# Letting GpSimd take q×E, k/E, the carried state's masked copy and the squares, under a newly drawn order of steps

## The chip, the cores and the metric

The kernel runs on one core of a Trainium2 chip. The metric is the time of one execution on the device in microseconds, as a median of runs. A core has five engines that run side by side, each in its own order: TensorE (PE in the profile), VectorE (DVE), ScalarE (ACT), GpSimd (POOL) and SyncE (SP), which here only issues transfers.

## The reference

Two layers, one after the other. The first is a recurrence over 768 places in 4 batches and 8 heads of width 48, with a complex decay for each place and channel:

```python
mag = np.sqrt(a_re * a_re + a_im * a_im)
scale = np.minimum(mag, 0.999) / (mag + 1e-06)
a_re_n, a_im_n = (a_re * scale, a_im * scale)
for t in range(S):                                  # S = 768
    new_re = ar * S_re - ai * S_im
    new_im = ar * S_im + ai * S_re
    kv = np.einsum('bhd,bhe->bhde', k[:, :, t], v[:, :, t])
    S_re, S_im = (new_re + kv, new_im)
    y[:, :, t] = np.einsum('bhd,bhde->bhe', q[:, :, t], S_re)
```

The second takes y as x, 3072 rows of 384 channels, through a gated feed-forward layer with a gated residual:

```python
g = x @ w_gate                                      # 384 to 1536
gelu = 0.5 * g * (1.0 + erf(g * inv_sqrt2))
ffn_out = gelu * (x @ w_val) @ w_out                # 1536 to 384
res_gate = 1.0 / (1.0 + np.exp(-(x @ w_res)))
return x + res_gate * ffn_out
```

## The kernel before

The sequence is cut into 6 chunks of 128 places, which lie on the 128 partitions. A unit is one chunk of one or two batches; there are 14 units (0 to 13), of one chunk each for units 0, 1, 12 and 13 and of two for the others. For each unit three functions record steps.

`prepare` loads a_re, a_im, q, k and v by SyncE's queue (`load`, L374). From a_re and a_im it makes the logarithm of the decay and its angle: `ln`, `exp`, `tai` (t times a_im, L398), `sq` (the square, L400 or L402), `lnb`, `la`, `lh`, `ll`, and `atan`. The running sums over the 128 places are products on TensorE with a triangle of ones (`cumL`, `cumT`, L360). To keep float32 accuracy each summand is split into a half-precision part and a rest: `lh` and `ll`, `th` and `tl` (L444). ScalarE turns the sums into E (`pexpE`) and its inverse Ei (`pexpI`), and with `round`, `fr`, `abs` and `sin` into cosine and sine, CS. Then `qe` makes q×E and k×Ei (k over E), in bfloat16 (L470), and `feat` multiplies both with CS to the features of width 96 (L475). These are transposed, on TensorE with a copy out of PSUM (`peT`, L492, and `cpT`, L334 or L335) in units 0 to 7, by SyncE's queue (`dT`, L484) later. The angle's last row goes from chunk to chunk by a transfer on GpSimd's queue (`carry`, L432 and L438).

`attend` makes the query-key products (`qk`, L522), masks them (`am`, L525), multiplies with v and adds the carried state (`av`, L534 and L536), and copies the result to x. The carried state is updated: `kv` on TensorE, `U` (L552) adds the old state, and two masked copies are made, Gb in bfloat16 (L554) for the next product and Gf in float32 (L559) for the next update.

`forward` is the second layer: x transposed, `gv` (L592), `gelu` (L597) on ScalarE, `h` (L598) on VectorE, `res` (L607), `tanh` (L609), `out` (L618), `ot` (L622), and `otx` (L625), the sum with x, before the store (L627).

The steps are not issued as they are recorded. All 1450 have a number; ORDER lists them in the order of issue, over all units and engines, and PLACE gives the engine of those steps that may run on more than one (`place` takes the default where PLACE is silent). Each engine runs its steps in the order of that list. ScalarE's functions come from three table sets; `run` loads a set when the next step in the list needs another one (L639).

VectorE and GpSimd take turns for the kinds in PORT: such a step waits for the last PORT step of the other engine that stands before it in the list. These are the lines that do it:

```python
if t.kind in PORT and t.eng in ("DVE", "POOL"):
    other = turn.get("POOL" if t.eng == "DVE" else "DVE")
    if other is not None:
        after(ins, other)
    turn[t.eng] = ins
```

Kinds that read PSUM (`am`, `h`, `ot`, `fr`, `U`, and the copies out of PSUM) aren't in PORT.

Buffers: 23 float32 buffers of 128×768 (`wd`) serve all loads and the steps of `prepare`; a step that takes one waits until its last user is done. PSUM has 8 banks.

Of the kernel before, what the change touches and what calls it, by code (L numbers as in the profile page):

```python
# [15 lines left out]
OP = mybir.AluOpType  # L16
# [14 lines left out]
    24: "DVE", 33: "DVE", 36: "POOL", 40: "DVE", 50: "DVE", 51: "DVE", 53: "ACT", 59: "DVE", 105: "DVE", 114: "DVE",  # L31
    116: "POOL", 121: "DVE", 132: "ACT", 134: "ACT", 145: "ACT", 190: "DVE", 191: "DVE", 205: "ACT", 213: "DVE", 223: "DVE",
    225: "ACT", 227: "DVE", 236: "DVE", 245: "DVE", 305: "DVE", 306: "DVE", 322: "POOL", 323: "POOL", 330: "DVE", 340: "DVE",
    342: "ACT", 344: "DVE", 353: "DVE", 363: "DVE", 422: "DVE", 435: "ACT", 438: "POOL", 439: "POOL", 454: "ACT", 456: "DVE",
    460: "DVE", 538: "DVE", 554: "POOL", 555: "POOL", 562: "DVE", 572: "DVE", 574: "ACT", 576: "DVE", 595: "DVE", 670: "POOL",
    671: "POOL", 678: "DVE", 688: "DVE", 692: "DVE", 783: "DVE", 786: "POOL", 787: "POOL", 804: "DVE", 808: "DVE", 827: "DVE",
    902: "POOL", 903: "POOL", 929: "DVE", 933: "DVE", 1014: "POOL", 1015: "POOL", 1022: "DVE", 1094: "DVE", 1121: "ACT",
    1124: "ACT", 1125: "POOL", 1132: "DVE", 1143: "DVE", 1160: "DVE", 1232: "POOL", 1233: "POOL", 1251: "ACT", 1257: "DVE",
    1263: "DVE", 1298: "DVE", 1304: "DVE", 1324: "ACT", 1329: "DVE", 1338: "ACT", 1396: "POOL", 1397: "POOL", 1410: "ACT",
    1416: "DVE", 1448: "DVE",  # L40
}
ORDER = [
# [145 lines left out]
def kernel(  # L188
# [13 lines left out]
    nc = tc.nc  # L202
# [122 lines left out]
    on = {"DVE": nc.vector, "POOL": nc.gpsimd, "ACT": nc.scalar}  # L325
    add = plan.add

    def place(default):

        return PLACE.get(len(plan.steps), default)  # L330
# [23 lines left out]
    Gf, Gb = [None] * B, [None] * B  # L354
# [145 lines left out]
    def attend(p):  # L500
# [12 lines left out]
        for i, (b, c) in enumerate(units[p]):  # L513
# [26 lines left out]
            if c < NC - 1:  # L540
# [8 lines left out]
                src = dk  # L549
# [120 lines left out]
```

## Time and profile before

| | |
|---|---|
| median of 3 runs | 260.99 us (260.36 to 261.66) |
| profiled execution | 260.65 us |
| its span in the profile | 258.9 us |
| busy: TensorE, VectorE, ScalarE, GpSimd | 224.1, 225.6, 210.1, 97.9 us |
| mean granted TensorE clock | 0.993 |
| table loads on ScalarE | 37, 47.5 us |

Between the span and the time of the execution lie 1.75 us. In rows of groups, the number behind x is the count, then come busy us, mean ns of one, and the idle time of the engine just before them with what ended it. In the timeline and the chain, a row begins with its start and its length in us.

### The profile page before, as it was taken

Reading aid. Unit: us, or ns where it says so; the run is one execution under the profiler, and the core shown is the slowest. Engines: PE = TensorE matmul, PEld = TensorE weight load, DVE = VectorE, ACT = ScalarE, POOL = GpSimd, SP = SyncE. Lnnn points to the kernel's source line nnn. Section 1 sums busy time; section 2 is a strip of 40 time slices with the busy share of each in tenths; the row PEclk is TensorE's granted clock in tenths of the full one; section 3 lists DMA queues with packets and bytes.
Section 4 is the critical chain, followed back from the end, with each engine's and each line's share of the span. In section 5 each row is a group of like instructions: output and inputs, shape, how many; then the busy total and the mean of one; then the engine's idle time right before and its main releaser. Section 6 shows DMA issues by size and latency. Waiting matters only on the chain.

```text
span 258.9 us, 6345 instructions
## 1 busy us (share of the span) xinstructions
PE 224.1 (87%) x2415; PEld 175.8 (68%) x2415; DVE 225.6 (87%) x405; ACT 210.1 (81%) x345; POOL 97.9 (38%) x124
## 2 busy tenths in 40 slices
PE   0405567879999899999999999999999999999992
PEld 0102456759786787787878778778777887878871
DVE  2699899999999999999999999999999985918452
ACT  5899999999999999999999999999798743141430
POOL 1212439968151286453567615464020120102001
PEclk9999999799999999999999999999999999999999
DMA  8999999999978999998998988989499459112011
GB/s 139 187 187 186 187 183 180 217 198 194 186 158 169 189 172 166 193 174 173 196 171 179 175 174 160 190 150 163 132 119 225 102 110 144 44 48 91 18 63 62
DMA packets 162174, 39.83 MB, mean 154 GB/s; under 512 B 155616, under 2 KB 162144, under 8 KB 162144
## 3 DMA queue, kind: packets, MB, share of 16 engines
q1 hardware_dynamic: 157696, 35.53, 78.8%
q0 software_dynamic: 4448, 3.90, 9.5%
q8 instruction: 19, 0.31, 0.5%
q14 instruction: 11, 0.09, 0.1%
HBM read 31.26 MB, written 4.72 MB: 139 GB/s over the span
## 4 chain that ended last, share of the span: by engine, by line
PE 60%; DVE 19%; ACT 6%; DMA 5%; issue 4%; POOL 3%; SPq 1%; DVEq 0%; ACTq 0%; POOLq 0%
PE pb L592 28%; PE pb L618 17%; PE pb L607 4%; PE pb L360 3%; DVE am L525 3%; PE pb L522 3%; DVE h L598 2%; DMA ai<-in_a_im_dram 2%; DVE KT L335 2%; DMA t<-fr 2%; ACT L639 2%; PE pb L534 1%; DVE fQ L475 1%; DMA ar<-in_a_re_dram 1%; PE pb L492 1%
## 5 line engine op out<-in xcount | busy, mean ns | idle before, releaser
L597 ACT ACTIVATE h<-pb 128x512 bf16<-128x512 f32 (+1 forms) x84 | 41.6, 546 | 24.8 <-PE pb L592 24.5
L592 PE MATMUL pb<-xT,wg 128*128 128x256 bf16 (+1 forms) x504 | 58.2, 259 | 1.8 <-DVE Gb L554 1.2
L592 PE MATMUL pb<-xT,wv 128*128 128x256 bf16 (+1 forms) x504 | 58.0, 257 | 0.0
L618 PE MATMUL pb<-wo,h 128*128 128x384 bf16 x288 | 56.9, 326 | 0.3 <-DVE U L552 0.3
L598 DVE SCALAR_TENSOR_TENSOR h<-h,pb 128x512 bf16<-128x512 bf16 (+1 forms) x84 | 48.6, 603 | 3.3 <-ACT h L597 2.4
L625 POOL TENSOR_TENSOR ot<-ot,x 128x384 f32<-128x384 f32 x20 | 18.2, 914 | 84.1 <-ACT h L597 20.2
L592 PEld LDWEIGHTS <-wg 128*128 128x128 bf16 x504 | 43.7, 99 | 8.5 <-issue 1.6
L639 ACT ACT_TABLE_LOAD x37 | 47.5, 1283 | 1.3 <-PEq L654 0.7
L592 PEld LDWEIGHTS <-wv 128*128 128x128 bf16 x504 | 42.1, 98 | 6.6
L618 PEld LDWEIGHTS <-h 128*128 128x128 bf16 x288 | 26.2, 97 | 13.5 <-issue 0.4
L525 DVE TENSOR_TENSOR am<-pb,mask 128x512 bf16<-128x512 f32 x48 | 32.0, 681 | 1.2 <-PE pb L522 1.2
L622 DVE SCALAR_TENSOR_TENSOR ot<-sg,pb 128x384 f32<-128x384 f32 x24 | 13.1, 547 | 13.2 <-PE pb L618 11.5
L360 PE MATMUL pb<-lh,ut_hf 128*128 128x384 f16 x24 | 9.0, 373 | 16.5 <-DVE lh L406 16.5
L522 PE MATMUL pb<-QT,KT 96*128 96x128 bf16 x192 | 18.5, 226 | 3.2 <-DVE QT L335 2.3
L522 PEld LDWEIGHTS <-KT 96*128 96x128 bf16 x192 | 13.7, 101 | 7.1 <-issue 3.5
L444 POOL TENSOR_TENSOR tl<-t,th 128x768 fp32r<-128x768 f32 (+1 forms) x11 | 16.6, 1512 | 3.8 <-DVE t L398 1.4
L609 ACT ACTIVATE sg<-pb 128x384 f32<-128x384 f32 x24 | 11.6, 496 | 8.0 <-PE pb L607 7.9
L335 POOL CAST th<-t 128x768 f16<-128x768 f32 (+1 forms) x10 | 7.6, 762 | 23.0 <-ACT t L426 8.4
L360 PEld LDWEIGHTS pb<-ll,ut_one 128*128 128x128 f32 x24 | 5.4, 224 | 16.1 <-DVE ll L408 15.8
L398 POOL TENSOR_TENSOR t<-t,ai 128x768 f32<-128x768 f32 (+1 forms) x8 | 12.9, 1613 | 8.4 <-DVE lh L406 6.3
L607 PE MATMUL pb<-wr,xT 128*128 128x384 bf16 x72 | 15.3, 326 | 0.2 <-DVE xT L335 0.2
L559 POOL TENSOR_TENSOR Gf<-U,M 96x384 f32<-96x384 f32 x11 | 9.2, 844 | 13.6 <-DVE fQ L475 6.2
(90 smaller groups left out, 471.6 us busy)
## 6 DMA issues: line engine op xcount, KB each, us to landing
ar<-in_a_re_dram SPq DMA_DIRECT2D x24, 192.0 KB, 4.6
ai<-in_a_im_dram SPq DMA_DIRECT2D x24, 192.0 KB, 4.6
q<-in_q_dram SPq DMA_DIRECT2D x24, 192.0 KB, 4.1
k<-in_k_dram SPq DMA_DIRECT2D x24, 192.0 KB, 4.5
vf<-in_v_dram SPq DMA_DIRECT2D x24, 192.0 KB, 4.4
out_dram<-ot SPq DMA_DIRECT2D x24, 192.0 KB, 2.2
wg<-in_moe_w_gate_dram POOLq DMA_DIRECT2D x6, 192.0 KB, 4.9
wv<-in_moe_w_val_dram POOLq DMA_DIRECT2D x6, 192.0 KB, 6.8
```

Source lines behind the costliest of these rows:

```text
L360: nc.tensor.matmul(out=bank.tile, lhsT=ones, rhs=x[:, i * DM:(i + 1) * DM], start=(j == 0), stop=(j == 1))
L444: add(e10, "tl", lambda: on[e10].tensor_tensor(out=F("tl"), in0=F("t"), in1=F("th"), op=OP.subtract), [s["t"], s["th"]], [s["tl"]], n)
L522: nc.tensor.matmul(out=ap.tile[:, h, :], lhsT=kT.tile[0:DD, u * H // 2 + h, :], rhs=qT.tile[0:DD, u * H // 2 + h, :], start=True, stop=True)
L525: add("DVE", "am", lambda u=u, am=am, ap=ap: nc.vector.tensor_tensor(out=am.tile[:, u * H // 2:(u + 1) * H // 2, :], in0=ap.tile, in1=mask ...
L592: nc.tensor.matmul(out=o_.tile[:, u, :], lhsT=w_[:, k_, (2 * m + u) * 128:(2 * m + u + 1) * 128], rhs=s["xT"].tile[:, k_, 0:n].rearrange(" ...
L597: add("ACT", "gelu", lambda gp=gp, hv=hv: nc.scalar.activation(out=hv(), in_=gp.tile, func=AF.Gelu), [gp], [hh], n, "G")
L598: add("DVE", "h", lambda vp=vp, hv=hv: nc.vector.scalar_tensor_tensor(out=hv(), in0=hv(), scalar=0.5, in1=vp.tile, op0=OP.mult, op1=OP.mul ...
L607: nc.tensor.matmul(out=rp.tile, lhsT=s["xT"].tile[:, k_, i, :], rhs=wr[:, k_, :], start=(k_ == 0), stop=(k_ == KF - 1))
L618: nc.tensor.matmul(out=op_.tile, lhsT=s["h2"].tile[:, k_, i * 128:(i + 1) * 128], rhs=wo[:, k_, :], start=(k_ == 0), stop=(k_ == NF - 1))
L622: add("DVE", "ot", lambda i=i, op_=op_, ot=ot: nc.vector.scalar_tensor_tensor(out=ot.tile, in0=sg[i].tile, scalar=1.0, in1=op_.tile, op0=O ...
L625: add(e8, "otx", lambda i=i, ot=ot, e8=e8: on[e8].tensor_tensor(out=ot.tile, in0=ot.tile, in1=s["x"].tile[:, i].rearrange("p h d -> p (h d ...
L639: plan.run(ORDER, lambda table: nc.scalar.preload_act_table_set(ACT_SETS[table]), after)
```

## The change

PLACE may now name GpSimd for three more kinds of steps, which only VectorE (or ScalarE, for the squares) ran before: `qe`, `Gb`, and `sq`. ORDER and PLACE are new lists. The steps themselves, their number and their numbering stay.

```diff
-        if place("ACT") == "ACT":
+        e13 = place("ACT")
+        if e13 == "ACT":
             act("sq", lambda: nc.scalar.activation(out=F("s"), in_=F("t"), func=AF.Square), [s["t"]], [s["s"]])
         else:
-            add("DVE", "sq", lambda: nc.vector.tensor_tensor(out=F("s"), in0=F("t"), in1=F("t"), op=OP.mult), [s["t"]], [s["s"]], n)
+            add(e13, "sq", lambda: on[e13].tensor_tensor(out=F("s"), in0=F("t"), in1=F("t"), op=OP.mult), [s["t"]], [s["s"]], n)
...
         for g, src, mag in (("Q", "q", "E"), ("K", "k", "Ei")):
-            add("DVE", "qe", lambda g=g, src=src, mag=mag: nc.vector.tensor_tensor(
+            e12 = place("DVE")
+            add(e12, "qe", lambda g=g, src=src, mag=mag, e12=e12: on[e12].tensor_tensor(
                 out=T(g + "e")[:, 0:n * H].rearrange("p x u d -> p (x u d)"), in0=flat(T(src), n),
                 in1=P2(mag).rearrange("p c m -> p (c m)"), op=OP.mult), [s[src], s[mag]], [s[g + "e"]], n)
...
-                add("DVE", "Gb" if c else "Gb0", lambda nb=nb, src=src, mb=mb: nc.vector.tensor_tensor(
+                e11 = place("DVE") if c else "DVE"
+                add(e11, "Gb" if c else "Gb0", lambda nb=nb, src=src, mb=mb, e11=e11: on[e11].tensor_tensor(
                     out=nb.tile[0:DD], in0=src.tile[0:DD], in1=mb(), op=OP.mult), [src, s["M"]], [nb])
```

What the new lists move, counted over all units (before to after, a wide step being one over two chunks):

| steps | VectorE | GpSimd | ScalarE |
|---|---|---|---|
| q×E and k/E, wide | 20 to 6 | 0 to 14 | |
| q×E and k/E, narrow | 8 to 7 | 0 to 1 | |
| Gb | 16 to 4 | 0 to 12 | |
| Gf | 1 to 2 | 11 to 10 | |
| squares, wide and narrow | 4 to 3 | 0 to 3 | 10 to 8 |
| sums with x | 4 to 13 | 20 to 11 | |
| t×a_im | 6 to 9 | 8 to 5 | |
| th, wide and narrow | 1 to 4 | 10 to 5 | 3 to 5 |
| tl | 3 to 3 | 11 to 11 | |
| casts of v | 2 to 1 | 8 to 7 | 4 to 6 |
| copies of transposes out of PSUM | 26 to 29 | | 6 to 3 |
| table loads | | | 37 to 36 |

The first entries of ORDER show how the start differs. Before, SyncE's first loads are a_re of unit 1, a_re and a_im of unit 0, a_im of unit 1, then unit 3's a_re; after, half of unit 3's a_re comes first and the other half third:

```diff
-    97, 16, 17, 98, 294, 102, 21, 181, 22, 23, 178, 103, 24, 179, 25, 104, 180, 105, 26, 34, 293, 27, 115, 28, 35, 295, 29, 116,
+    294, 16, 293, 97, 17, 98, 21, 296, 102, 22, 295, 303, 23, 103, 24, 104, 25, 105, 106, 304, 26, 107, 19, 178, 179, 180, 181,
...
```

More of the change, by code (lines that the diff above doesn't have):

```diff
@@ L30 @@
 PLACE = {
[L31 to L38, printed above, removed]
@@ L39 @@
-    1263: "DVE", 1298: "DVE", 1304: "DVE", 1324: "ACT", 1329: "DVE", 1338: "ACT", 1396: "POOL", 1397: "POOL", 1410: "ACT",
-    1416: "DVE", 1448: "DVE",
+    24: "DVE", 35: "POOL", 36: "POOL", 40: "DVE", 50: "DVE", 51: "DVE", 53: "ACT", 59: "DVE", 105: "DVE", 114: "ACT",
+    116: "POOL", 121: "DVE", 131: "DVE", 190: "DVE", 203: "DVE", 213: "DVE", 217: "POOL", 223: "DVE", 227: "DVE", 230: "ACT",
+    236: "DVE", 245: "DVE", 305: "DVE", 306: "DVE", 330: "DVE", 333: "POOL", 342: "ACT", 344: "DVE", 345: "ACT", 356: "POOL",
@@ new lines @@
+    363: "DVE", 366: "POOL", 402: "DVE", 408: "DVE", 435: "ACT", 438: "POOL", 439: "POOL", 450: "POOL", 456: "DVE", 460: "DVE",
+    472: "POOL", 538: "DVE", 539: "POOL", 551: "DVE", 554: "ACT", 555: "POOL", 565: "POOL", 572: "DVE", 576: "DVE", 577: "ACT",
+    585: "DVE", 595: "DVE", 598: "POOL", 599: "DVE", 640: "DVE", 654: "DVE", 667: "ACT", 671: "POOL", 678: "DVE", 681: "POOL",
+    682: "POOL", 688: "DVE", 692: "DVE", 695: "ACT", 704: "POOL", 711: "DVE", 714: "POOL", 750: "DVE", 786: "POOL", 787: "POOL",
@@ new lines @@
+    797: "POOL", 798: "POOL", 804: "DVE", 806: "ACT", 808: "DVE", 809: "ACT", 811: "ACT", 827: "DVE", 830: "POOL", 831: "DVE",
+    866: "DVE", 872: "DVE", 899: "ACT", 903: "POOL", 914: "POOL", 921: "ACT", 929: "DVE", 932: "POOL", 939: "DVE", 942: "POOL",
+    978: "DVE", 999: "POOL", 1011: "ACT", 1014: "POOL", 1015: "POOL", 1022: "DVE", 1025: "POOL", 1026: "POOL", 1033: "ACT",
+    1044: "POOL", 1050: "DVE", 1108: "DVE", 1121: "ACT", 1124: "ACT", 1125: "POOL", 1132: "DVE", 1135: "POOL", 1136: "POOL",
@@ L41 @@
+    1145: "ACT", 1154: "POOL", 1163: "POOL", 1198: "DVE", 1204: "DVE", 1232: "ACT", 1233: "POOL", 1240: "DVE", 1244: "POOL",
+    1257: "DVE", 1298: "DVE", 1304: "DVE", 1313: "DVE", 1324: "ACT", 1325: "POOL", 1329: "DVE", 1376: "DVE", 1385: "DVE",
+    1386: "POOL", 1396: "ACT", 1397: "POOL", 1405: "POOL", 1410: "ACT", 1448: "DVE",
 }
 ORDER = [
[62 rows of a table removed]
[62 rows of a table added]
 ]
```

122 rows, old and new, of the table ORDER are left out of this document.

## The prediction

> **What bounds the kernel now.** I read the page first: the busy times, then the rows of the span in 40 slices.
>
> ```profile
> span 258.9 us, 6345 instructions
> PE 224.1 (87%) x2415; PEld 175.8 (68%) x2415; DVE 225.6 (87%) x405; ACT 210.1 (81%) x345; POOL 97.9 (38%) x124
> PE   0405567879999899999999999999999999999992
> DVE  2699899999999999999999999999999985918452
> ACT  5899999999999999999999999999798743141430
> POOL 1212439968151286453567615464020120102001
> ```
>
> Three engines are full for most of the span: VectorE and ScalarE from 6 us on, TensorE later, and TensorE alone at the end. GpSimd has room. The windows view cuts the same span into stretches of 13 us; each engine's column is its busy us:
>
> ```profile
> 0.00:13.00 13.00, 3.21 (x6) 1.34 (x7) 5.93 (x16) 8.88 (x12) 2.67 (x13) 1.00 1.13 163
> 13.00:26.00 13.00, 4.08 (x11) 1.87 (x10) 12.29 (x19) 12.53 (x19) 2.31 (x3) 1.00 1.44 186
> 26.00:39.00 13.00, 8.01 (x59) 6.05 (x58) 11.98 (x22) 12.53 (x21) 5.31 (x7) 1.00 1.30 185
> 39.00:52.00 13.00, 10.14 (x121) 8.36 (x119) 12.76 (x26) 12.98 (x21) 11.87 (x17) 0.87 1.21 199
> 91.00:104.00 13.00, 12.38 (x163) 9.88 (x161) 13.00 (x23) 12.91 (x19) 9.99 (x10) 1.00 0.97 166
> 221.00:234.00 13.00, 13.00 (x120) 10.26 (x118) 7.27 (x13) 3.96 (x7) 1.18 (x2) 1.00 0.12 39
> ```
>
> TensorE stands for 26.6 us of the first 52, while ScalarE stands for 5.1, nearly all of it in the first 13. So the end is set in two parts: how late TensorE's work is fed in the first 100 us (by ScalarE and VectorE), and then TensorE's remaining work. What counts is therefore the **lead**: at a TensorE step, the work of ScalarE (or VectorE) that must be done before it, less the TensorE work that stands before it. The largest lead, plus the time the feeder stood, plus all of TensorE's work, is the earliest end.
>
> For the sums I price each step by its row. TensorE's:
>
> ```profile
> 208.84 3.27 PE pb L592 x30
> 249.66 1.95 PE pb L618 x12
> ```
>
> This is the chain: 0.109 us for a 256-column product and 0.163 us for a 384-column one. With such prices all of TensorE's list is 207 us; the page's 224 also counts the time in which results still run out. ScalarE's and VectorE's records overlap a little: two small ScalarE steps take 0.94 us together where one shows 0.52 (below). With 0.08 off each, the lists sum to 210 us for ScalarE and 220 us for VectorE, beside the page's 210.1 and 225.6.
>
> In the list of before, ScalarE's largest lead stands at the first query-key product of unit 5. Ahead of it stand 143 ScalarE steps and 16 table loads, 91.1 us, and 52.4 us of TensorE work: a lead of 38.7 us. The timeline has that place:
>
> ```profile
> 95.39 1.00 ACT L334 COPY QT<-pb 96x1024 bf16<-96x1024 bf16 x1
> 96.44 0.38 PE L522 MATMUL pb<-QT,KT 96*128 96x128 bf16 x4 [0.29 <-ACT QT L334]
> 251.94 2.11 PE L618 MATMUL pb<-wo,h 128*128 128x384 bf16 x12
> ```
>
> TensorE does wait there for ScalarE's copy, which ends at 96.4: 91.1 of work and 5.3 of standing. 96.4 + (207 - 52.4) = 251.0; TensorE's last product ends at 254.05, so 3 us are lost later. VectorE is almost as tight: its largest lead is 32.6 us (98.1 ahead of the transposes of unit 6, at 65.5 of TensorE). By the windows it has stood 9 us by then, and my sum is some 2 us short there (2% of 98, as 220 is of 225.6): 32.6 + 11.4 = 44.0, beside ScalarE's 38.7 + 5.3 = 44.0. **Two feeders bind alike**; relief for one alone brings nothing.
>
> **The change, part by part.** These are the prices of what moves.
>
> ```profile
> L470 DVE TENSOR_TENSOR Ke<-k,Ei 128x768 bf16<-128x768 f32 x10 | 9.5, 949 | 0.2 <-ACT Ei L417 0.2
> L554 DVE TENSOR_TENSOR Gb<-U,M 96x384 bf16<-96x384 f32 x16 | 8.8, 547 | 0.0
> L625 DVE TENSOR_TENSOR ot<-ot,x 128x384 f32<-128x384 f32 x4 | 2.2, 556 | 0.2
> L444 POOL TENSOR_TENSOR tl<-t,th 128x768 fp32r<-128x768 f32 x9 | 14.8, 1643 | 3.2 <-DVE t L398 1.4 <-PE pb L536 0.8 <-DVE Gb L554 0.7
> L398 POOL TENSOR_TENSOR t<-t,ai 128x768 f32<-128x768 f32 x6 | 10.9, 1817 | 8.4 <-DVE lh L406 6.3 <-DVE la L404 1.6 <-DMA ai<-in_a_im_dram 0.5
> L559 POOL TENSOR_TENSOR Gf<-U,M 96x384 f32<-96x384 f32 x11 | 9.2, 844 | 13.6 <-DVE fQ L475 6.2 <-DVE Qe L470 3.4 <-DVE Ke L470 2.0
> L625 POOL TENSOR_TENSOR ot<-ot,x 128x384 f32<-128x384 f32 x20 | 18.2, 914 | 84.1 <-ACT h L597 20.2 <-DVE ot L622 18.2 <-issue 15.8
> L335 POOL CAST th<-t 128x768 f16<-128x768 f32 x8 | 6.6, 824 | 14.7 <-DVE Ke L470 5.2 <-DMA t<-fr 3.8 <-PE pb L546 2.7
> L639 ACT ACT_TABLE_LOAD x37 | 47.5, 1283 | 1.3 <-PEq L654 0.7
> L334 ACT COPY QT<-pb 96x1024 bf16<-96x1024 bf16 x4 | 4.0, 1006 | 0.2 <-PE pb L492 0.2
> ```
>
> VectorE's list loses 14 wide q×E or k/E steps (14 × 0.949 = 13.3) and a narrow one (0.6), and 12 Gb (12 × 0.547 = 6.6). It gains 9 sums with x (9 × 0.556 = 5.0) and some 3.5 us of casts, copies and t×ai. With the overlap taken off, VectorE's list falls from 220.4 to 210.5. GpSimd takes on 14 × 1.64 = 23.0 for the wide steps, 12 × 0.84 = 10.1 for Gb, and 3 squares, some 4.2. It gives up 9 sums with x (8.2), 5 wide casts of th (4.1), and others: 98 becomes 117 us. That GpSimd writes bf16 from two f32 inputs is in no row: between 0.82 (one input) and 1.82 (two); I take 1.64, the nearest in operands. ScalarE's sum stays (210.1 to 209.4, 36 table loads for 37), but its order doesn't.
>
> GpSimd and VectorE take turns: a step of a kind in PORT waits for the last such step of the other engine before it in the list. While GpSimd multiplies, VectorE can only do steps that read PSUM. I went through the list after, stretch by stretch: wherever GpSimd's turns stand between two of VectorE's, the VectorE steps between them that need no turn cover them, but for 2.9 us in all (before: 2.1). So the slower engine's time is hidden in the list. In the trace of before such cover held well; VectorE's waits for GpSimd are few:
>
> ```profile
> DVE tl L444 <- POOL mr L335: 0.9, 1, 0.9
> DVE fw L461 <- POOL tl L444: 0.8, 1, 0.8
> DVE tl L444 <- POOL th L335: 0.7, 1, 0.7
> DVE Qe L470 <- POOL ot L625: 0.5, 1, 0.5
> ```
>
> Now the leads of the new list. At the same product of unit 5, ScalarE has 89.3 us ahead: one table load less (1.28) and three copies of transposes less (2.8), 2.2 us of other steps more. TensorE has 55.0 ahead, 2.6 more (two more parts of an output product, 1.3, and a few sums and gate products). The lead there is 34.3 instead of 38.7. The largest is now 34.8, at the transposes of unit 7 (119.8 less 85.0), and 34.6 at TensorE's 131. So ScalarE's part is **-3.9 us**. VectorE's largest lead falls from 32.6 to 29.7, **-2.9 us**, and from TensorE's 100 on it is 27 or less, where it was 27 to 32.
>
> A rule bears on the loads' price. The Trainium skill (ScalarE: Activation LUTs, section "What ACT_TABLE_LOAD costs") gives 1283 ns and a drain of about 1380 ns for every switch; by that the 16 loads ahead of unit 5 would take 22 us more, and the one load saved 2.66. The trace has no room for it: below, a load starts at 7.93 and the next step at 9.22.
>
> The first 15 us get worse. The first rows of the timelines:
>
> ```profile
> 3.85 0.52 ACT L395 ACTIVATE la<-ar 128x384 f32<-128x384 f32 x1 [1.83 <-DMA ar<-in_a_re_dram]
> 4.91 0.52 ACT L395 ACTIVATE la<-ar 128x384 f32<-128x384 f32 x1 [0.55 <-DMA ar<-in_a_re_dram]
> 5.47 0.94 ACT L396 ACTIVATE t<-la 128x384 f32<-128x384 f32 x2
> 6.04 0.56 DVE L398 TENSOR_TENSOR t<-t,ai 128x384 f32<-128x384 f32 x1 [2.60 <-ACT t L396]
> 7.93 1.28 ACT L639 ACT_TABLE_LOAD   x1
> 9.22 0.94 ACT L426 ACTIVATE t<-t 128x384 f32<-128x384 f32 x2
> ```
>
> The first two loads land 1.06 us apart, which is 192 KB at the windows' 186 GB/s. The new list loads half of unit 3's a_re first and third, so a_re of units 0 and 1 come second and fourth, and the first a_im fifth: about 3.85 + 4 × 1.06 = 8.1 us instead of 6.0. Followed step by step with these rows, ScalarE ends the exponential of unit 2 at 17.3 us having worked 11.3: 6.0 us of standing, against 4.6 before. I add **+1.3 us** (from 0.3, if the fifth load lands a place sooner, to 2.5, if one weight load of 192 KB cuts in).
>
> The **sum**: ScalarE 34.8 + 5.3 + 1.3 = 41.4; VectorE 29.7 + 11.4, and with up to 0.8 more of uncovered turns, 41.1 to 41.9; both were 44.0. So -2.3 us (-2.1 to -2.9). The last steps keep their kind (an output product, VectorE's product and sum, a store), so the tail stays. The profiled execution took 260.65 us, its span and 1.75 around it; the runs' median is 260.99. 260.65 - 2.3 = **258.3 us**, of the span some 256.6.
>
> **The rivals.** *VectorE is held by GpSimd* (slower). Each moved product takes GpSimd 0.69 us longer than VectorE (1.643 less 0.949), each Gb 0.30. Up to the place of the largest lead 8 products and 3 Gb have moved: 6.5 us. Where a turn begins late, for an operand that ScalarE has not delivered, its cover has passed, and VectorE stands. In 12 stretches with products the cover is on average only 0.8 us longer than the turn. Two thirds of 6.5 uncovered gives 258.3 + 4.3 = 262.6; it is slower than before from 3.6 us on. For it: the margins, and VectorE's lead has no room. Against it: 2.9 us of such waits in the four rows above. The Trainium skill (GPSIMD Engine Reference, section 4.1) says the same as a rule: elementwise products of two inputs belong on VectorE, GpSimd being about twice as slow; the rows have 1.7 times. I give this 0.20.
>
> *No change* (about 260.2): the first loads cost 2.5 us instead of 1.3, and 0.7 of turns come on top. The new list brings two weight loads forward in the first 25 us, when the queue is full; for it speaks the DMA share of 1.13 to 1.44 in the first windows. 0.23.
>
> *A larger gain* (256.8): the 3 us that TensorE loses after 96 us shrink by half, since VectorE's lead falls by up to 10 us late. Against it: after 221 us TensorE is full anyway. This is part of the 0.57 for faster, with the forecast.
>
> **How the numbers follow.** Forecast and larger gain have 0.57, within 0.5% has 0.23, slower 0.20; 0.5%, 1.3 us, is about what a measurement of this kernel can tell from no change. The range goes from 255.3 (a gain of 3 beyond the largest sum) to 262.9, just past the rival's 262.6; about 0.07 is left out below and 0.12 above.
>
> **What would show it.** Right: VectorE's busy time near 215 us, GpSimd's near 117, k/E on GpSimd at 1.6 to 1.8 us; the copy of unit 5's transposes no longer what TensorE waits for at 96 us; TensorE's last product at some 251.7; ScalarE's first a_re step of the second unit at about 7 us. Wrong: waits of VectorE for GpSimd of over 6 us in the first 110 us, with TensorE's idle time in them; or ScalarE's standing over 7.5 us by 90 us.

## The result and the profile after

The changed kernel takes 259.3 us (median of 5 runs, 258.27 to 259.62); the kernel before on the same chip takes 260.99 (5 runs). The ratio is 0.9935, with a 95% interval of 0.9912 to 0.9958: 1.7 us less. The profiled execution took 258.27 us, at the fast end of its runs; the forecast for it was 258.3. The difference of 1 us between it and the median comes up again below.

The page of the changed kernel, its busy times and slices:

```profile
span 256.4 us, 6321 instructions
PE 220.2 (86%) x2415; PEld 174.1 (68%) x2415; DVE 216.7 (85%) x391; ACT 209.3 (82%) x350; POOL 117.5 (46%) x132
PE   0060871879999999999999999989999999999993
DVE  2669999999999999999999989979987786817364
ACT  2899999999999999999999999899799944223340
POOL 1045068797246379866647676543561131400000
```

VectorE has 8.9 us less to do (216.7 for 225.6), GpSimd 19.6 more, ScalarE 0.8 less. TensorE's slices are emptier at the start (0060871 for 0405567). The windows, with the columns of the prediction's, show by how much:

```profile
0.00:13.00 13.00, 0.00 (x0) 0.10 (x1) 5.96 (x16) 7.16 (x11) 1.24 (x11) 1.00 1.15 164
13.00:26.00 13.00, 4.60 (x9) 1.66 (x8) 10.68 (x20) 12.64 (x20) 5.87 (x9) 1.00 1.31 187
26.00:39.00 13.00, 9.94 (x80) 7.07 (x80) 12.35 (x22) 12.51 (x25) 5.11 (x7) 1.00 1.16 195
39.00:52.00 13.00, 7.28 (x93) 6.25 (x94) 13.00 (x23) 12.94 (x18) 10.97 (x16) 0.74 1.16 199
52.00:65.00 13.00, 11.63 (x168) 9.69 (x166) 12.74 (x28) 12.39 (x22) 10.19 (x10) 1.00 1.26 206
91.00:104.00 13.00, 13.00 (x171) 10.68 (x170) 12.84 (x23) 12.93 (x20) 11.40 (x9) 1.00 1.03 194
```

In the first 52 us TensorE stands for 30.2 us, 3.6 more than before. From 65 us on it stands no more, but for 0.6 us near 170 and the tail: 13.00 of 13 in the window from 91, where it was 12.38. Its busy time for the same 2415 products is also 3.9 us less (220.2 for 224.1), nearly all of it in the first 65 us (33.5 for 37.0). Busy counts the time in which results run out, hides stops too short to show as standing, and grows where products run at half clock; these were not taken apart.

So the idle column alone doesn't hold the gain, and a better measure is the lead as it was in fact: the start of a TensorE product in the timeline, less all TensorE work ahead of it. That work is priced by the usual time from one start to the next at full clock: 0.109 us for a product of 256 columns, 0.163 for 384, 0.055 for 128, 0.027 for 48, and 0.34 for a pair of `lh` and `ll` or `th` and `tl`. It comes to 208.6 us where the prediction had 207, so a lead is good to about 1 us. Time lost at half clock counts into it. In the kernel before it was 40.6 us at 58, 40.8 at 64, 44.1 at 100 and 45.3 at the last product; in the changed kernel it is 42.0 at 64, 42.3 at 100, 43.5 at 172 and 43.6 at the last product. So the start is some 1 us worse, and from 64 us on 1.6 us are lost, where before 4.5 were. TensorE's last product ends 1.7 us sooner; the other 0.8 of the 2.5 us by which the span is shorter lie behind it, and are told under the prediction's size below.

The view of waits shows what is left: the waits for VectorE's `lh`, `fK` and `x`, all ahead of 56 us, hold 27.2 of the 31.6 us for which TensorE stands in the first 65.

```profile
PE pb L364 <- DVE lh L411: 20.2, 2, 14.1
PE pb L498 <- DVE fK L481: 4.7, 1, 4.7
PE pb L585 <- DVE x L339: 2.3, 3, 1.5
```

The wait for ScalarE's copy QT at unit 5's query-key product, on which the forecast rested, is gone. The last rows that answer to those shown of before are the first steps' and the last product's, from the timelines:

```profile
4.83 0.52 ACT L399 ACTIVATE la<-ar 128x384 f32<-128x384 f32 x1 [2.81 <-DMA ar<-in_a_re_dram]
6.94 0.52 ACT L399 ACTIVATE la<-ar 128x384 f32<-128x384 f32 x1 [1.58 <-DMA ar<-in_a_re_dram]
8.07 0.56 DVE L402 TENSOR_TENSOR t<-t,ai 128x384 f32<-128x384 f32 x1 [4.62 <-DMA ai<-in_a_im_dram]
11.68 1.28 ACT L646 ACT_TABLE_LOAD   x1
16.86 0.84 ACT L400 ACTIVATE t<-la 128x768 f32<-128x768 f32 x1
250.26 2.11 PE L625 MATMUL pb<-wo,h 128*128 128x384 bf16 x12
```

And the prices of what was moved, from the groups by line with different shapes kept apart:

```profile
L476 POOL TENSOR_TENSOR Ke<-k,Ei 128x768 bf16<-128x768 f32 x8 | 14.5, 1816 | 1.8 <-DVE Qe L476 0.8 <-ACT Ei L422 0.8 <-issue 0.2
L476 POOL TENSOR_TENSOR Qe<-q,E 128x768 bf16<-128x768 f32 x6 | 10.9, 1818 | 6.5 <-ACT E L421 3.3 <-DVE M L339 1.8 <-DVE ll L413 1.2
L449 POOL TENSOR_TENSOR tl<-t,th 128x768 fp32r<-128x768 f32 x8 | 13.2, 1648 | 2.9 <-DVE ll L413 1.6 <-DVE th L339 1.2
L561 POOL TENSOR_TENSOR Gb<-U,M 96x384 bf16<-96x384 f32 x12 | 9.9, 827 | 24.6 <-DVE ot L632 5.1 <-DVE Qe L476 4.9 <-DVE fK L481 4.4
```

A wide product on GpSimd takes 1.82 us, not 1.64; a Gb takes 0.83, for 0.84 forecast.

### The profile page after: what moved, and what is told of

It is laid out like the page before. It is cut to its first block, busy times and chain, and to the rows that moved or that the text cites. A ratio compares the mean times of both kernels' runs of the same rounds, so it can differ in the third digit from the quotient of the medians.

```text
span 256.4 us, 6321 instructions
## 1 busy us (share of the span) xinstructions
PE 220.2 (86%) x2415; PEld 174.1 (68%) x2415; DVE 216.7 (85%) x391; ACT 209.3 (82%) x350; POOL 117.5 (46%) x132
## 4 chain that ended last, share of the span: by engine, by line
PE 71%; DVE 13%; ACT 8%; DMA 4%; issue 2%; SPq 1%; DVEq 0%; ACTq 0%
PE pb L599 34%; PE pb L625 16%; PE pb L498 5%; PE pb L364 5%; PE pb L614 4%; PE pb L528 3%; ACT L646 3%; DVE am L531 2%; DMA KT<-fK 2%; DMA ai<-in_a_im_dram 2%; DVE fr L457 2%; PE pb L542 1%; PE pb L540 1%; PE pb L552 1%; ACT t L431 1%
## 5 line engine op out<-in xcount | busy, mean ns | idle before, releaser
L599 PE MATMUL pb<-xT,wg 128*128 128x256 bf16 (+1 forms) x504 | 57.5, 257 | 0.0
L599 PEld LDWEIGHTS <-wg 128*128 128x128 bf16 x504 | 43.3, 98 | 6.5
L561 POOL TENSOR_TENSOR Gb<-U,M 96x384 bf16<-96x384 f32 x12 | 9.9, 827 | 24.6 <-DVE ot L632 5.1
L476 POOL TENSOR_TENSOR Ke<-k,Ei 128x768 bf16<-128x768 f32 (+1 forms) x9 | 15.5, 1725 | 7.2 <-ACT fw L464 5.4
L528 PE MATMUL pb<-QT,KT 96*128 96x128 bf16 x192 | 17.9, 219 | 0.2 <-DVE KT L339 0.2
L449 POOL TENSOR_TENSOR tl<-t,th 128x768 fp32r<-128x768 f32 (+1 forms) x11 | 15.9, 1449 | 3.1 <-DVE ll L413 1.6
L399 ACT ACTIVATE la<-ar 128x768 f32<-128x768 f32 (+1 forms) x14 | 10.6, 759 | 4.9 <-DMA ar<-in_a_re_dram 4.8
L498 PE MATMUL pb<-ident,fK 128*128 128x128 bf16 x112 | 10.0, 246 | 4.7 <-DVE fK L481 4.7
L476 POOL TENSOR_TENSOR Qe<-q,E 128x768 bf16<-128x768 f32 x6 | 10.9, 1818 | 6.5 <-ACT E L421 3.3
```

The costliest lines, as they stand in the source:

```text
L449: add(e10, "tl", lambda: on[e10].tensor_tensor(out=F("tl"), in0=F("t"), in1=F("th"), op=OP.subtract), [s["t"], s["th"]], [s["tl"]], n)
L476: add(e12, "qe", lambda g=g, src=src, mag=mag, e12=e12: on[e12].tensor_tensor(out=T(g + "e")[:, 0:n * H].rearrange("p x u d -> p (x u d)") ...
L498: nc.tensor.transpose(out=tp.tile[:, h, :], in_=s[g].tile[:, i * H + h], identity=ident)
L528: nc.tensor.matmul(out=ap.tile[:, h, :], lhsT=kT.tile[0:DD, u * H // 2 + h, :], rhs=qT.tile[0:DD, u * H // 2 + h, :], start=True, stop=True)
L599: nc.tensor.matmul(out=o_.tile[:, u, :], lhsT=w_[:, k_, (2 * m + u) * 128:(2 * m + u + 1) * 128], rhs=s["xT"].tile[:, k_, 0:n].rearrange(" ...
```

## The experiments

They are told in four groups. All differences in us are between medians and the changed kernel's 259.3; every kernel was also compared with the kernel before on its own chip (260.5 to 260.7 us), and the ratio is given.

### Order without placing, and placing without order

The first kernel is the one before with the new ORDER; q×E, k/E, Gb and the squares stay on VectorE or ScalarE, and the other steps stay where they were.

```diff
 ORDER = [
-    97, 16, 17, 98, 294, 102, 21, 181, 22, 23, 178, 103, 24, 179, 25, 104, 180, 105, 26, 34, 293, 27, 115, 28, 35, 295, 29, 116,
+    294, 16, 293, 97, 17, 98, 21, 296, 102, 22, 295, 303, 23, 103, 24, 104, 25, 105, 106, 304, 26, 107, 19, 178, 179, 180, 181,
...
```

> The new ORDER with the PLACE of before: q×E, k/E, Gb and the squares are VectorE's and ScalarE's again. Theory A (two feeders bind alike, and the end is the larger lead plus TensorE's 207 us): VectorE's lead becomes 33.6, with 11.4 of standing 45.0, where the changed kernel has some 41.5: 3.5 us over its 259.3, so 262.8 us. Rival B (the gain comes from the order alone, through ScalarE and its table loads): 259.3 us. Rival C (the gain comes from VectorE's relief alone): as before the change, 261.0 us.

It took 287.43 us, ratio 1.1043 (1.1012 to 1.1074). Every theory missed by over 24 us. The second kernel is the changed kernel with the old ORDER, the same lines of the diff the other way round.

> The ORDER of before with the new PLACE. Theory A: VectorE's lead falls to 29.8, but ScalarE's stays, 39.8 at unit 8, with 5.3 of standing 45.1 instead of 44.0: 261 to 262 us. Rival B (order alone): 261.0 us, as before. Rival C (VectorE's relief alone): 259.3 us or less. If the cover of GpSimd's turns was a matter of the list, VectorE waits for GpSimd for much longer here than the 4.7 us of the changed kernel, and the time lies over 262.

It took 284.14 us, ratio 1.09 (1.0871 to 1.093). Here the three theories missed by 22 us or more too, and only the last sentence came true: VectorE waits for GpSimd for much longer. Rows of the waits, of the first kernel and then of the second:

```profile
ACT h L600 <- PE pb L595: 38.9, 25, 6.2
DVE Gb L557 <- POOL ot L628: 2.7, 3, 1.3
```

```profile
ACT h L604 <- PE pb L599: 26.1, 18, 7.5
ACT s L408 <- POOL s L407: 9.0, 2, 4.9
DVE la L409 <- POOL Ke L476: 4.7, 1, 4.7
```

VectorE's waits for GpSimd add up to 17 us in the first and 28 in the second, without the one at the start of every kernel for a constant; in the changed kernel they are 4.7. In the second, ScalarE itself waits 9 us for two squares that GpSimd makes too late. The windows of the first show what that does; the columns are those of above:

```profile
91.00:104.00 13.00, 12.09 (x128) 10.16 (x127) 11.85 (x18) 11.34 (x19) 5.12 (x6) 1.00 1.08 174
156.00:169.00 13.00, 11.26 (x122) 8.73 (x120) 11.59 (x21) 9.52 (x16) 5.37 (x5) 1.00 0.62 112
```

No engine is full: TensorE, VectorE and ScalarE each stand one to three and a half us of 13. What follows: the order and the placing are one thing. The lead, a sum over one feeder, knows the work of each engine but not the waits between the engines. For lists that don't fit each other these waits are 17 and 28 us, where the forecast's whole gain was 2.3. The sum alone said 261 to 263 for the mixtures; that it came near for the two lists as they were made goes with their few such waits, 3.1 us before and 4.7 after.

### The moved steps put back, in the new order

First all 15 q×E and k/E that GpSimd has, then all 12 Gb, each alone. Both edits change entries of PLACE; two of the lines, the first from one kernel and the second from the other:

```diff
-    116: "POOL", 121: "DVE", 131: "DVE", 190: "DVE", 203: "DVE", 213: "DVE", 217: "POOL", 223: "DVE", 227: "DVE", 230: "ACT",
+    116: "POOL", 121: "DVE", 131: "DVE", 190: "DVE", 203: "DVE", 213: "DVE", 217: "DVE", 223: "DVE", 227: "DVE", 230: "ACT",
...
-    236: "DVE", 245: "DVE", 305: "DVE", 306: "DVE", 330: "DVE", 333: "POOL", 342: "ACT", 344: "DVE", 345: "ACT", 356: "POOL",
+    236: "DVE", 245: "DVE", 305: "DVE", 306: "DVE", 330: "DVE", 333: "POOL", 342: "ACT", 344: "DVE", 345: "ACT", 356: "DVE",
```

> The changed kernel, with the 15 q×E and k/E steps of GpSimd back on VectorE, in the new order. Theory A: VectorE's lead grows to 36.9 us, at TensorE's 128; with 11.4 of standing 48.3 instead of 41.5: 266 us. Rival (elementwise products belong on VectorE, since GpSimd needs 1.8 us where VectorE needs 0.95): 259.3 us or less.

269.31 us, ratio 1.0324 (1.0288 to 1.0361): 10.0 us more, where theory A had 6.7. The rival, that these products belong on VectorE, falls for this list.

> The changed kernel, with the 12 Gb of GpSimd back on VectorE. Theory A: VectorE's lead grows from 29.7 to 30.7 us early and by up to 5 us late, where it has room: 0.6 to 1.4 us more, 260.2 us. Rival (Gb's place is of no account, since the end is set in the first 57 us, where only one of these Gb stands): 259.3 us.

262.63 us, ratio 1.0071 (1.0046 to 1.0096): 3.3 us more. Theory A had 0.9 and the rival nothing, so both missed. The busy times of the two, in that order:

```profile
PE 225.2 (84%) x2415; PEld 176.1 (66%) x2415; DVE 228.3 (85%) x406; ACT 210.4 (79%) x350; POOL 91.5 (34%) x117
```

```profile
PE 224.0 (86%) x2415; PEld 177.0 (68%) x2415; DVE 221.9 (85%) x403; ACT 209.8 (80%) x350; POOL 108.0 (41%) x120
```

VectorE gets 11.6 and 5.2 us more work, and the end comes 10.0 and 3.3 us later: 0.86 and 0.63 us for each us of VectorE. In the new order most of what is added to VectorE arrives at the end, and the moved steps are worth that much there. The Trainium skill (GPSIMD Engine Reference, section 4.1) says that elementwise products of two inputs belong on VectorE because GpSimd is about twice as slow. The duration agrees: 1816 ns stand against 949, 1.9 times. Followed in this list, the rule costs 10.0 us, since GpSimd stands for more than half of the span and VectorE doesn't. But the list was drawn for products on GpSimd; the kernel before, which has them on VectorE under a list of its own, is 1.7 us slower than the changed one.

Where the time is lost can be counted by the lead as it was in fact. With Gb back it is 43.8 us at 64, 44.8 at 100 and 48.2 at 247. With the products back it is 45.2 at 64, 49.3 at 127 and 54.2 at 188. So it isn't one place that is late: the loss grows all along.

### Small work added to a feeder, early and late

By the forecast's sums VectorE has slack late (its lead is 27 us from TensorE's 100 on, where the largest is 29.7), and after the result a second theory stood beside that: only the first 57 us count, where the chain of waits of the changed kernel runs through VectorE. Four kernels add a block of small useless steps behind one step of ScalarE or VectorE:

```diff
+    first = plan.steps[804].fn
+
+    def longer():
+        ins = first()
+        for _ in range(20):
+            nc.vector.memset(spare, 0.0)
+        return ins
+
+    plan.steps[804].fn = longer
     plan.run(ORDER, lambda table: nc.scalar.preload_act_table_set(ACT_SETS[table]), after)
```

On ScalarE 16 small copies stand in place of the 20 fills. ScalarE early, VectorE early, ScalarE late, VectorE late:

> The changed kernel with 16 small copies added on ScalarE behind the exponential of unit 4 (some 33 us into the span), about 2.4 to 3 us of work that nobody uses. Theory A (ScalarE is a feeder that binds): the time grows by nearly all of it, 261.5 to 262.3 us. Rival (VectorE alone binds): 259.3 us, and up to 1 us more.

> The changed kernel with 20 small memsets added on VectorE at some 33 us of the span, about 2.5 to 3.5 us of work that nobody uses. Theory A (VectorE is a feeder that binds there): the time grows by nearly all of it, 261.5 to 262.5 us. Rival (ScalarE alone binds): 259.3 us, and up to 1 us more.

> The same 16 copies on ScalarE behind the exponential of unit 11, some 136 us into the span. Theory A: ScalarE's lead there (34.6 at TensorE's 131) is as large as its largest, 34.8, so the time grows by 1.5 to 2.8 us, to 261 to 262 us. Rival D (the end is set in the first 57 us, and from then on TensorE alone counts): 259.3 us.

> The same 20 memsets on VectorE behind a copy of unit 7's transposes, some 131 us into the span. Theory A: VectorE's lead is 25 there, 4 us or more below its largest, so nothing is lost: 259.3 us, 0.3 more at most. Rival (three engines are full, so each microsecond counts anywhere): 261.5 us or more.

They took 264.63, 264.04, 265.74 and 264.54 us (ratios 1.0154, 1.0132, 1.0198 and 1.0149, each to within 0.003): 5.3, 4.7, 6.4 and 5.2 more. The blocks were longer than meant; they lasted 4.7 to 4.8 us on ScalarE and 4.4 on VectorE. Late costs as much as early: that VectorE has room late falls, and so does that the first 57 us alone count.

The differences are larger than the blocks, and not all of them is the blocks'. By the lead, TensorE in the two kernels with a late block is already 1.8 us later at 136 us, ahead of the block, than in the profile of the changed kernel (44.3 and 44.4 for 42.5); the section on TensorE's clock comes back to this. From there to the last product ScalarE's late block loses 6.5 us and VectorE's 5.0, the changed kernel 1.1. So some 5.4 and 3.9 us belong to the blocks. Behind ScalarE's, TensorE also runs at half clock from about 145 to 148 us.

The timelines show how a block arrives: VectorE's late block and the TensorE step behind it, then ScalarE's late block and the TensorE step behind that:

```profile
136.87 4.41 DVE L652 MEMSET spare<- 128x96 f32 x20
143.88 1.47 PE L600 MATMUL pb<-xT,wg 128*128 128x256 bf16 x12 [3.85 <-DVE am L532]
```

```profile
138.53 4.82 ACT L652 CAST spare<-mask 128x96 f32<-128x96 bf16 x16
145.32 0.59 PE L529 MATMUL pb<-QT,KT 96*128 96x128 bf16 x4 [4.10 <-ACT h L605]
```

TensorE is full in the changed kernel there (13.00 of 13 us), yet a stop of 4.41 us of VectorE stops it for 3.85: it is not more than 0.6 us ahead of what VectorE must hand it next. The first, early block of VectorE stopped it as long:

```profile
37.49 1.03 PE L499 MATMUL pb<-ident,fQ 128*128 128x128 bf16 x8 [4.31 <-DVE fQ L482]
```

A busy column of 13.00 of 13 is no slack. What was still open was whether work in crumbs is taken up by VectorE's short idle times. The last two kernels put one fill behind every second of VectorE's steps, 20 in all, early or late; the early one's edit:

```diff
+    def longer(fn):
+        def both():
+            ins = fn()
+            nc.vector.memset(spare, 0.0)
+            return ins
+        return both
+
+    for n in [206, 125, 323, 51, 126, 129, 209, 55, 213, 59, 136, 62, 654, 219, 541, 227, 223, 221, 542, 442]:
+        plan.steps[n].fn = longer(plan.steps[n].fn)
```

> The changed kernel with 20 small fills added on VectorE, one behind every second of its steps between about 22 and 45 us; the 20 together took 4.41 us as one block. No step finds VectorE held for more than 0.22 us at a time. In the trace of the changed kernel VectorE is full from 38 to 55 us and the chain of waits runs through it there. Theory E (the end is set in the first 57 us, by VectorE): some 3.5 to 4.4 us more, 262.8 to 263.7. Rival (the blocks cost time because they were blocks, and TensorE is only a few PSUM banks ahead; spread work goes into the gaps): 259.3 to 260.5.

> The same 20 fills one behind every second of VectorE's steps between about 139 and 162 us, where the block of 4.41 us cost 5.2. In that stretch VectorE stands for 1 us in 13 and TensorE is full. Theory E (from about 65 us on TensorE sets the end, and VectorE's standing there takes up small work; the block cost time only because it held VectorE longer than TensorE's banks last): 259.3 to 260.5. Rival (each microsecond of VectorE counts wherever it lies): 262.8 to 263.7.

They took 259.46 (ratio 0.9953, 0.9937 to 0.9969) and 260.08 us (0.9986, 0.9975 to 0.9997). That doesn't decide it, because the dose was too small. VectorE's timeline in the early one:

```profile
43.32 0.14 DVE L650 MEMSET spare<- 128x96 f32 x1
43.37 0.29 DVE L340 COPY xT<-pb 128x384 bf16<-128x384 bf16 x1
43.58 0.94 DVE L482 TENSOR_TENSOR fK<-Ke,CS 128x1536 bf16<-128x1536 bf16 x1
```

With a fill between two steps, the next step starts 0.10 us later and its own record is 0.05 us shorter, so one fill delays VectorE by 0.05 us, where a fill in the block cost 0.22. The 20 together are 1.0 us, and nothing of 4 us could be seen. The fills also came later than meant, at 28 to 52 and 153 to 175 us. The fK above starts 0.33 us later than in the changed kernel (43.25), behind 13 fills of 0.05; the rest went into idle times of VectorE.

The late kernel is the slower of the two, and slower than the changed kernel by its ratio (the intervals lie apart). Its fills don't show as the reason: its lead is 43.8 at 64 us, 1.8 above the changed kernel's and long before the first of them, and from 136 us on it loses 1.2 us where the changed kernel loses 1.1. So the late crumbs cost 0.1 us of 1.0 by this count, which is within its error: a hint that they are taken up, and no test. The two kernels give no support to the theory that the early stretch decides.

### The start, and TensorE's clock

One kernel gives the first loads back their old places (a_re and a_im of units 0 and 1 ahead of unit 3's), in the new order otherwise:

```diff
-    294, 16, 293, 97, 17, 98, 21, 296, 102, 22, 295, 303, 23, 103, 24, 104, 25, 105, 106, 304, 26, 107, 19, 178, 179, 180, 181,
+    16, 97, 17, 98, 293, 294, 21, 102, 295, 22, 103, 296, 23, 24, 104, 25, 105, 106, 303, 304, 26, 107, 19, 178,
+    179, 180, 181, 305, 34, 99, 108, 306, 27, 28, 29, 115, 319, 116, 18, 117, 109, 118, 35, 188, 36, 100, 643, 189,
...
```

> The changed kernel with the first 27 entries of its ORDER in another sequence: SyncE loads a_re and a_im of units 0 and 1 first and unit 3's a_re after them, and ScalarE takes unit 3's first logarithm behind the two short ones. The second table set is loaded at 10.7 us instead of 11.7. Rival D (the end of the changed kernel is set in the first 57 us): the whole 1.0 us comes back, 258.3 us. Theory A in its first form (the largest lead is unit 7's, at 126 us, and the first microseconds delay it as much): also 1.0 us, 258.3. If the first loads are of no account, since VectorE and the transfers set the next steps: 259.3 us.

259.1 us, ratio 0.9935 (0.9921 to 0.9949), the same as the changed kernel's: the order of the first loads doesn't account for the loss at the start. Its timelines, ScalarE's second table load and two of TensorE's waits:

```profile
10.79 1.28 ACT L645 ACT_TABLE_LOAD   x1
43.74 1.04 PE L497 MATMUL pb<-ident,fK 128*128 128x128 bf16 x8 [4.56 <-DVE fK L480]
53.16 0.34 PE L584 MATMUL pb<-ident,x 128*128 128x128 bf16 x3 [0.25 <-DVE x L338]
```

The same two waits of the changed kernel:

```profile
44.25 1.04 PE L498 MATMUL pb<-ident,fK 128*128 128x128 bf16 x8 [4.65 <-DVE fK L481]
53.27 0.34 PE L585 MATMUL pb<-ident,x 128*128 128x128 bf16 x3 [0.25 <-DVE x L339]
```

The table load comes 0.9 us sooner, unit 2's transposes 0.5, TensorE's step behind the copy x at 53 us only 0.1. In between, TensorE starts from a stand of over 4 us and runs at half its clock. (The clock column shows 1.00 ahead of the first change on record, which can't be right: eight transposes take 1.08 us at 29.03 and 0.62 at 33.55 in the changed kernel, and in the one before 1.03 at 37.22 and 0.62 at 42.30. So TensorE starts at half its pace in both, and the mean clocks count that time as full.) So the last kernel keeps TensorE at work through that stand, with 64 products more that are written over:

```diff
                 def run(...):
...
+                    if p == 2 and i == 1 and g == "K":
+                        for h in range(64):
+                            nc.tensor.transpose(out=tp.tile[:, h % H, :], in_=ident, identity=ident)
```

> The changed kernel with 64 transposes of the identity ahead of unit 2's first transposes, into the same PSUM bank, where TensorE stands from 39.3 to 44.25 us and the granted clock falls to 0.5 till 47 us. They leave the results as they are. If the half clock costs what it seems (four groups of 8 transposes at 0.87 us instead of 0.44): 1 to 1.7 us less, 257.6 to 258.3 us. If TensorE has slack there, since VectorE sets the steps till 56 us (the chain of waits runs through VectorE there): 259.3 us.

259.87 us, ratio 0.9968 (0.9951 to 0.9986): no gain. The timeline shows why the full clock brings nothing there: with it TensorE comes to the products `kv` at 46.78 us instead of 47.41, then waits 0.74 us for VectorE's copy QT, and starts the next query-key products at 47.88 instead of 47.65. The windows of 3 us, with the granted clock third from the end, of the changed kernel, of this one, and of the kernel with fills late (whose list and work are the same as the changed kernel's up to its first fill at 153 us):

```profile
45.00:48.00 3.00, 3.00 (x45) 2.90 (x43) 3.00 (x6) 2.98 (x4) 2.88 (x5) 0.64 1.09 187
57.00:60.00 3.00, 3.00 (x47) 2.89 (x45) 2.78 (x7) 2.96 (x6) 2.11 (x3) 1.00 1.25 204
```

```profile
45.00:48.00 3.00, 2.02 (x37) 1.86 (x36) 3.00 (x6) 2.99 (x3) 2.49 (x6) 1.00 1.13 189
57.00:60.00 3.00, 3.00 (x36) 2.99 (x35) 2.78 (x6) 2.26 (x4) 2.42 (x4) 0.61 1.07 161
```

```profile
45.00:48.00 3.00, 3.00 (x32) 2.90 (x31) 3.00 (x6) 2.98 (x4) 2.67 (x6) 0.50 1.14 190
57.00:60.00 3.00, 3.00 (x37) 3.00 (x35) 2.97 (x6) 1.83 (x4) 2.71 (x4) 0.62 1.22 209
```

The clock did stay at 1.00 where it had been 0.64. But in this kernel, and in the one with late fills too, the clock dips at 56 to 60 us, which it doesn't in the changed kernel's profiled execution. There the dip costs 1.5 us: from the transposes of x at 55 us to the twelve gate products behind unit 3's transposes it takes 4.44 us in the changed kernel (55.06 to 59.50) and 5.91 in the one with late fills (55.67 to 61.58). Their two profiled executions lie 1.8 us apart (258.27 and 260.1). Both kernels with a late block, which also run the changed kernel's list up to there, show the dip too. So the changed kernel's own slower executions may well have it, and its median may be 1 us above its profile for this. That is argued, not shown, as only one execution of it was profiled.

The mean clocks on record bear it out in part. Of the changed kernel's five runs, those of 259.3 and 259.41 us have 0.979 and 0.980, the profiled one 0.985; the difference is about one more stretch of 3.4 us at half clock. But the slowest, 259.62, has 0.987. Of the twelve runs with late fills, the six below 0.98 have a mean of 260.35 us and the six others 259.83: 0.5 us, not 1.5.

## Why the prediction was right, and where it was not

**What bounds.** That TensorE is fed late in the first 100 us and that the rest is TensorE's work held: the changed kernel's TensorE stands no more after 65 us, but for 0.6 us. "Two feeders bind alike" was put to no test of its own in the kernel before; in the new one, blocks of either feeder cost their full length.

**The size.** The largest lead was forecast at 41.4 us. Counted in the timeline it is 42.0 at 64 us and 43.6 at the end. The span came out at 256.4 for 256.6, but luck has a part in that: two errors cancel. TensorE's last product ends at 252.37 for the forecast 251.7, 1.7 us sooner than before and not 2.35. The tail behind it, which the forecast left as it was since "the last steps keep their kind", is 0.8 us shorter, 4.04 us for 4.83. The last steps did not keep their engine: before, GpSimd makes the last sum but one with x, and after, VectorE does. These rows show that sum before, GpSimd's closing steps before (the view of the program's last line: count, then the shortest, middle and longest in ns, and first and last start in us), and the sum after:

```profile
253.53 0.91 POOL L625 TENSOR_TENSOR ot<-ot,x 128x384 f32<-128x384 f32 x1 [16.68 <-DVE ot L622]
L665 POOLq DRAIN  x3: 46/155/4218, 253.5 to 258.6; - x3
251.71 0.56 DVE L632 TENSOR_TENSOR ot<-ot,x 128x384 f32<-128x384 f32 x1
```

GpSimd's closing step begins at 253.5 and lasts 4218 ns, to 257.72, which is 3.28 us behind the end of its sum, and the program's end comes 1.2 us later. In the changed kernel GpSimd has long been done, and the end hangs on the last store instead. The mixtures confirm that the place of a last sum sets this: the tail is 5.75 us with the old placing under the new order, where GpSimd makes the very last sum, and 3.99 with the new placing under the old order, where VectorE makes both. All other kernels made from the changed one have 4.03 to 4.17. With the tail as the profiles show it, 0.8 of the 1.7 us between the medians is this tail, and about 0.9 is left for what the forecast was about. In the profiles of the kernel with the old first loads and of the two with fills, which have the later dip of the clock, the lead is 43.3 to 44.2 at 64 us; there TensorE's last product ends at 253.58 to 254.28, for 254.05 before, and little more than the tail is gained.

**The place.** Wrong. The forecast put the largest lead at unit 7's transposes, with ScalarE ahead of them. In the trace 42.0 of 43.6 are reached by 64 us, and 0.8 of the rest comes at once near 170, where TensorE waits 0.65 us for ScalarE's Ei. The step that failed is the reading of leads as slack: that VectorE's late lead is 2 to 3 us smaller was taken to mean room for late work, and the late blocks show no such room (3.85 us of 4.41 arrive at TensorE at once). The lead counts only the work ahead; how far ahead each hand-over really lies, by its order in the list and the buffers between, it doesn't see.

**The head.** The walk through the first loads was right to 0.4 us: the first tai at 8.07 (8.1), the second a_re at 6.94 (7), unit 2's exponential ends at 17.70 (17.3). That its 1.3 us reach the end was wrong: with 0.9 us of it taken back, nothing came of it, since 0.4 of the 0.5 us that were left at 44 us were lost again by 53. ScalarE's standing by 90 us is 90 less 82.4, 7.6 us, just over the mark of 7.5 that was to show the forecast wrong; it had no consequence.

**The prices.** Busy times came as forecast: VectorE 216.7 (near 215), GpSimd 117.5 (117). A wide product was mis-sized at 1.64 us and takes 1.82, the upper end of the bounds: 14 × 0.17 = 2.4 us more, which GpSimd has to spare. The row that would have given it is that of t×a_im (1.817 in the trace of before), whose two inputs are float32 as well. `tl`, which the forecast took as the nearest in operands, subtracts a half-precision input.

**The slower rival.** VectorE was not held. Its waits for GpSimd, of the constant at the start apart, are these and a few below 0.5:

```profile
DVE t L402 <- POOL tl L449: 1.6, 1, 1.6
DVE Gf L566 <- POOL tl L449: 0.9, 1, 0.9
DVE tl L449 <- POOL th L339: 0.7, 1, 0.7
DVE fw L466 <- POOL Ke L476: 0.6, 1, 0.6
```

In the first 110 us they are 2.6 us (the mark was 6). The reading of the cover in the list, 2.9 us uncovered, came near: the waits are 4.7 us in all, 1.6 more than before. And the mechanism exists: with the old order it comes to 28 us.

**What stays open.** Putting back the two kinds costs 10.0 and 3.3 us, yet the whole change brings 1.7. The rest goes to what the new lists give to VectorE in return (8.5 us of sums with x, casts, copies and t×a_im by the prediction's prices), to the late start, and to what two lists made apart may differ in otherwise; these shares were not taken apart. So it isn't shown what share of the gain is the relief of VectorE; only the 0.8 us of the tail is traced to one step. Nor was it tried whether ScalarE or VectorE alone would have held the kernel before.

## What to carry to other kernels

Where a list written for one placing sets the order, judge the pair: half of the change, either half, cost 9 to 10 percent here, and neither sum of work told it. An engine of half the speed can be the right one for a step when it stands and the fast one is full, as the ten us for the products show here; what counts is that the fast engine has other work for the whole turn, and that can be read from the list. A busy engine is not an engine with work in store: test slack with a block of known length and see how much of it arrives. And ask of the last steps not only what they are but on which engine they lie.

## What the runs showed of the hardware

- On GpSimd a product of two float32 inputs of 128×768 takes 1.816 us into bfloat16 and 1.815 into float32. A subtraction of a half-precision from a float32 input into the float32 kind that TensorE reads (fp32r) takes 1.648, a square with one tile as both inputs 1.465; what of input, output and operation makes the difference was not separated.
- GpSimd's closing step ends 3.28 us behind its last sum in the kernel before and 3.27 in the one with the new order and the old placing. So a step of GpSimd among the very last lengthened the program by 0.8 and 1.7 us.
- TensorE's granted clock fell to 0.50 in its stand of 4.65 us ahead of 44.25 and, in the profiled execution of the changed kernel, was back at 1.00 from 48 us on. In the execution with late fills, the same list up to there, it fell a second time at 56 us, without a wait of TensorE of over 0.61 us before. The Trainium skill (TensorE: Matmul & The Clock Gate, part 1) says that activity is judged in windows of about 3.4 us which run free of the kernel, and that the count of slow products varies from run to run for that reason. The traces agree: the dip comes in one execution and not in another, and in their clock records every stretch at half clock that ends before the kernel does lasts 3.41 us or a whole multiple of it (6.83 in the changed kernel; 6.83 and 3.41 with late fills).
- A fill of 128×96 on VectorE costs 0.22 us behind another fill and 0.05 between other steps.
